# Super-step 0's transposed blocks from VectorE, and super-step 1's key products moved forward

## The chip, the cores and the metric

One core of one Trainium2 chip. The metric is the device time of the whole program in microseconds (us). The kernel before took 1152.81 us, the median of three runs (1151.03 to 1156.87).

## The reference

Three layers, one after the other. The first is a delta-rule attention with a state per batch and head (4 x 8 heads, 768 steps, head size 48):

```
k_n = k / (norm(k) + 1e-6)
for t in range(768):
    y[t]  = q[t] @ state
    v_old = k_n[t] @ state
    state = state + beta[t] * outer(k_n[t], v[t] - v_old)
```

The second takes the 3072 x 384 result through `relu(x @ w_in)**2 @ w_out` (inner size 2048), the third through `(silu(x @ w_gate) * (x @ w_val)) @ w_out2` (inner size 1536). The weights come as float64; the rest is float32.

## The kernel before, in words

The 768 steps are cut into 6 super-steps `J` of 128 steps, each of two chunks `c` of 64; of the four batches two lie on the two halves of the partitions and two are the halves `p` of the free axis, with 8 heads each. Inside a chunk the recurrence becomes a triangular system: `gram` products of the keys with themselves give M, an inverse of I+M is made, and products with it give `u`, from which come the outputs `y` and the next state (`ku`, `ks`). After super-step 0 a first expert loop (`moe1_h`, `moe1_o`, 16 rounds `m` for a super-step) runs on its 512 rows, and the work of the next super-step is put in between by a list of due times (`plan`, `spread`, `slot`).

Super-step 0 and the first part of super-step 1 are written out by hand (L1035 to L1135). The order of the `run(...)` lines is the order on TensorE, VectorE, ScalarE, GpSimd and SyncE (SP), whose queues are served in order. The names there:

- `gram0` (L392) makes the key products: 16 fp32 products a call. `gc` copies those of super-step 0; for super-step 1, `mb0` (L400, GpSimd) makes mask times beta in one of two buffers, `m0` (L407, VectorE) multiplies the product into it, `mout` sends it to memory, `tload` loads it back as T, and `inv` inverts T on GpSimd.
- For super-step 0, `din` brings the 32x32 blocks into T, `inv0` (L522, VectorE) inverts their 16x16 blocks, and `dout` (L430) transposes the result to ND, with the keys' rows on the partitions again.
- `dt` (L568) makes the transposed 16x16 blocks of ND by products with an identity: 32 products a call, four calls, one ScalarE copy each. `d1` and `d2` (L580, L590) merge two 16x16 blocks to a 32x32 inverse: 32 products a call each, a copy after `d1`, four small copies after `d2` that alternate between ScalarE and VectorE. `t11`, `m1`, `m2` then merge two 32x32 blocks to 64x64 (16 products a call); `dcopy` puts the blocks in place; `vn` scales v.
- `amm` makes the query-key products, `amask` (L487) masks them out of PSUM on VectorE.
- `sq` and `root` make the key norms of super-step 1.
- `conv(n)` does n steps of the conversion of an expert weight piece from float64: three VectorE steps a piece (L185, L187, L192), then a high part on ScalarE (L205) and a low part (L208). The low part of a piece is issued when the next piece is complete, or when it is needed. `PRE` is the count of steps done ahead of the loop; inside it the count aimed at is `PRE + int(3 * 0.65 * clock)`, with the clock counting two for a round.
- 20 products of a zero tile (L1082) run on TensorE while VectorE inverts.

PSUM banks in the start come from `bank(p)`: three of the pool `ps_a` for p = 0, three of `ps_t` for p = 1.

Of the kernel before, what the change touches and what calls it, by code (L numbers as in the profile page):

```python
# [8 lines left out]
F32 = mybir.dt.float32  # L9
F32R = mybir.dt.float32r  # L10
I32 = mybir.dt.int32
ACTF = mybir.ActivationFunctionType
# [9 lines left out]
def delta_attention_moe_moe2_kernel(  # L22
# [37 lines left out]
    nc = tc.nc  # L60
# [22 lines left out]
    ps_h = ctx.enter_context(tc.tile_pool(name="ps_h", bufs=2, space=bass.MemoryType.PSUM))  # L83
# [10 lines left out]
    lower = ap.tile([128, 1], F32, name="lower")  # L94
# [13 lines left out]
    own_w = wp.tile([128, 4 * DM], F32, tag="w", name="ND")  # L108
    own_h, own_l = (xp.tile([128, KD, TOK], F32, tag=t, name="own").rearrange("p k t -> p (k t)") for t in ("xh", "xl"))
    ND, BM = (t[:, 0:1024].rearrange("p (x t) -> p x t", t=32) for t in (own_w, own_l))  # L110
    ident = own_l[:, 1024:1152]
    tick = own_h[:, 512:640]
    TD = [t.rearrange("p (u h t) -> p u h t", u=2, h=8) for t in (own_w[:, 1024:1536], own_h[:, 0:512])]
    KB = {}
    T = ap.tile([128, 32, 32], F32, name="T")
    TMP = ap.tile([128, 240], F32, name="TMP")
# [44 lines left out]
    class Piece:  # L161
# [20 lines left out]
        def run(self):  # L182
            if is64:
                f, fi = self.f, self.f.bitcast(I32)
                nc.vector.tensor_scalar(out=fi, in0=fi, scalar1=3, scalar2=None, op0=ALU.logical_shift_left)  # L185
                yield
                nc.vector.scalar_tensor_tensor(  # L187
                    out=self.d[:, 1], in0=self.d[:, 1], scalar=-0x80000000, in1=fi,
                    op0=ALU.bitwise_and, op1=ALU.bitwise_or,
                )  # L190
                yield
                nc.vector.scalar_tensor_tensor(  # L192
                    out=self.d[:, 1], in0=self.d[:, 0], scalar=29, in1=self.d[:, 1],
                    op0=ALU.logical_shift_right, op1=ALU.bitwise_or,
                )
            yield
# [29 lines left out]
    def load_w1(pc, kd, eng=nc.sync):  # L226
        if (pc, kd) != LAST:
            load_piece((w_in, w_out)[kd], pc, kd == 1, raw1[pc, kd], eng)
            loaded[pc, kd, 0] = raw1[pc, kd]
# [92 lines left out]
    def bank(p, shape, name):  # L322

        if startup and p == 0:
            return ps_a.tile(shape, F32, tag="a", name=name)
        return ps_t.tile(shape, F32, tag="t", name=name)
# [88 lines left out]
    TT = T.rearrange("x t s -> x s t")  # L415
# [13 lines left out]

    def d_out():  # L430
        nc.vector.transpose(out=ND.rearrange("s x t -> s t x"), in_=T)

    def d_rest():

        for b0 in (32, 96):
            nc.gpsimd.memset(NTT[b0:b0 + 32, :, 0:32], 0.0)
        c_ = NTT[:, :, 32:64]
        nc.gpsimd.tensor_tensor(c_, c_, bF.unsqueeze(2).to_broadcast([128, 32, 32]), op=ALU.mult)
# [123 lines left out]
                )  # L562

    t11 = {}
    d_t = {}


    def d_tr(c, p):  # L568

        ps = bank(p, [128, 8, 16], "ps_dt")  # L570
        n = ND[:, 16 * c + 8 * p:16 * c + 8 * p + 8]
        for h in range(8):
            for b0 in range(0, 128, 32):
                nc.tensor.matmul(
                    ps[b0:b0 + 32, h], n[b0:b0 + 16, h], ident[b0:b0 + 16, b0:b0 + 16], start=True, stop=True
                )
        t = TD[c][:, p]
        nc.scalar.activation(out=t[:, :, 0:16], in_=ps, func=ACTF.Copy)
        d_t[c, p] = t

    def d_merge1(c, p):
        ps = bank(p, [128, 8, 16], "ps_d")
        t, n = d_t[c, p], ND[:, 16 * c + 8 * p:16 * c + 8 * p + 8]
        for h in range(8):
            for b0 in range(0, 128, 32):
                nc.tensor.matmul(ps[b0:b0 + 32, h], n[b0:b0 + 16, h], t[b0:b0 + 16, h, 0:16], start=True, stop=True)

        nc.scalar.activation(out=t[:, :, 16:32], in_=ps, func=ACTF.Copy, scale=lower)

    def d_merge2(c, p):  # L590
        ps = bank(p, [128, 8, 16], "ps_e")
        t, n = d_t.pop((c, p)), ND[:, 16 * c + 8 * p:16 * c + 8 * p + 8]
        for h in range(8):
            for b0 in range(0, 128, 32):
                nc.tensor.matmul(
                    ps[b0:b0 + 16, h], t[b0:b0 + 32, h, 16:32], n[b0:b0 + 32, h, 16:32], start=True, stop=True
                )
        for b0 in range(0, 128, 32):
            copy(b0 // 32 % 2, n[b0:b0 + 16, :, 16:32], ps[b0:b0 + 16])

    def copy(i, out, in_):

        if startup and i:
            nc.vector.tensor_copy(out, in_)
        else:
            nc.scalar.activation(out=out, in_=in_, func=ACTF.Copy)

    def tr11(J, c, p):
        t = TD[0][:, p] if J == 0 and c else ap.tile([128, 8, 32], F32, tag="tq", bufs=2, name="tq")
        if J == 0:  # L610
            ps = bank(p, [128, 8, 32], "ps_tq")
            for h in range(8):
                for b0 in (0, 64):
                    nc.tensor.matmul(
                        ps[b0:b0 + 32, h], ND[b0:b0 + 32, 16 * c + 8 * p + h], ident[b0:b0 + 32, b0:b0 + 32],
                        start=True, stop=True,
                    )
            for b0 in (0, 64):
                copy(b0 // 64, t[b0:b0 + 32], ps[b0:b0 + 32])
            t11[c, p] = t  # L620
            return
        for b0 in (0, 64):
            nc.vector.transpose(out=t[b0:b0 + 32], in_=NT[c][p][b0:b0 + 32, :, 0:32])
        t11[c, p] = t
# [137 lines left out]
    def do_y(J, c, p):  # L762
# [10 lines left out]
        "vn": (v_scale, 0),  # L773
        "nback": (n_back, 0), "t11": (tr11, 0), "m1": (merge1, 0.4), "m2": (merge2, 0.5), "ks": (ks, 0.8),
        "agram": (a_gram, 0.8), "u": (uu, 0.8), "ku": (do_ku, 0.8), "y": (do_y, 0.9),
        "fetch": (fetch_x, 0.01), "dt": (d_tr, 0), "d1": (d_merge1, 0.8), "d2": (d_merge2, 0.8),
        "sq": (k_squares, 0), "root": (k_root, 0), "gram0": (gram0, 0.9), "mb0": (mb0, 0), "m0": (m0, 0),
        "amm": (lambda J, c, p: a_gram(J, c, p, split=True), 0.8), "amask": (a_mask, 0),
        "gc": (g_copy, 0), "brows": (b_rows, 0), "din": (d_in, 0), "dout": (d_out, 0), "drest": (d_rest, 0),
# [223 lines left out]
    def run_all(names):  # L1003
        for n in names:
            run(n)
# [15 lines left out]
    def conv(n, lo=nc.vector):  # L1021

        conv_to(converted() + n, lo)

    P2 = range(2)
    WARM = 20
    mark = ap.tile([128, 1], F32, name="mark")

    def stage(w, J, c):
        run_all((w, J, c, p) for p in P2)  # L1030

    def merge16(w, c):
        run_all((w, c, p) for p in P2)
# [7 lines left out]
        out=BM, in_=BM, compare_op=ALU.is_gt, fill=0.0, base=0, pattern=[[1, 32], [-1, 32]], channel_multiplier=0  # L1041
    )
    nc.gpsimd.memset(AQT[32:64, :, 1], 0.0)
    nc.gpsimd.memset(tick, 0.0)
    run(("loadq", 0))
    run_all(("kt", 1, c) for c in P2)
    run_all(("kb", 1, c) for c in P2)
# [7 lines left out]
    for b0 in (0, 64):  # L1055
        nc.gpsimd.affine_select(
            out=mask[b0:b0 + 64], in_=mask[b0:b0 + 64], compare_op=ALU.is_ge, fill=1.0,
# [12 lines left out]
    run(("brows",))  # L1070
    run(("din",))
    stage("amm", 0, 0)
    run(("sq", 1, 0, 0))
    run(("inv0", range(14, 6, -1)))

    nc.vector.reduce_sum(lower, ident.rearrange("p (b z k) -> p z b k", z=2, k=16)[:, 1], axis=AX.XY)
    if WARM:

        nc.vector.memset(tick[:, 0:1], 0.0)
        spare = ps_h.tile([128, 128], F32, tag="h", name="ps_w")  # L1080
        for _ in range(WARM):
            nc.tensor.matmul(spare, tick, tick, start=True, stop=True)  # L1082
    run(("inv0", range(6, 0, -1)))

    nc.gpsimd.tensor_copy(mark, T[:, 0, 0:1])
    run(("dout",))
    merge16("dt", 0)
    stage("amask", 0, 0)
    run(("drest",))
    merge16("dt", 1)  # L1090
    run(("sq", 1, 0, 1))
    run(("sq", 1, 1, 0))
    merge16("d1", 0)
    run_all(("gram0", 1, 0, p) for p in P2)
    merge16("d1", 1)
    run(("sq", 1, 1, 1))
    merge16("d2", 0)
    run(("root", 1))
    run_all(("mb0", 1, 0, p, nc.gpsimd) for p in P2)
    merge16("d2", 1)  # L1100
    run(("vn", 0, 0, nc.vector))
    stage("t11", 0, 0)
    run(("dcopy", 0))
    run_all(("m0", 1, 0, p) for p in P2)
    run_all(("mout", 1, 0, p) for p in P2)
    stage("t11", 0, 1)
    run_all(("gram0", 1, 1, p) for p in P2)
    run_all(("mb0", 1, 1, p, nc.gpsimd) for p in P2)
    stage("m1", 0, 0)
    stage("m1", 0, 1)  # L1110
    stage("m2", 0, 0)
    run_all(("m0", 1, 1, p) for p in P2)
    run_all(("mout", 1, 1, p) for p in P2)
    run_all(("tload", 1, c) for c in P2)
# [1 line left out]
    load_w1(5, 0)  # L1116
    load_w1(5, 1)
    run(("inv", 1, 0, 1, nc.gpsimd))
    stage("m2", 0, 1)
    stage("u", 0, 0)  # L1120
    run(("dcopy", 1))
    conv(1)
    stage("amm", 0, 1)
    stage("y", 0, 0)
    conv(2)
# [174 lines left out]
```

## Time and profile before

| | |
|---|---|
| median of three runs | 1152.81 us |
| profiled execution | 1150.16 us |
| its span | 1148.4 us |
| TensorE busy | 1077.1 us (94%) |
| VectorE busy | 616.2 us (54%) |
| ScalarE busy | 383.0 us (33%) |
| GpSimd busy | 235.1 us (20%) |
| mean granted TensorE clock | 0.957 of full speed |

The profile is of one execution. Its page gives busy times, 40 slices of the span and the chain that ended last; the trace behind it is asked for one stretch, engine or line at a time. PE is TensorE's matmul, PEld its weight load, DVE VectorE, ACT ScalarE, POOL GpSimd, SP SyncE; L568 is line 568 of the kernel. Times of day are us from the start of the span. A busy engine is not an engine at its peak, and the idle time of an engine off the critical path costs nothing. "issue" is time in which an engine waited for nothing that the profile shows.

### The profile page before, as it was taken

Reading aid. Unit: us, or ns where it says so; the run is one execution under the profiler, and the core shown is the slowest. Engines: PE = TensorE matmul, PEld = TensorE weight load, DVE = VectorE, ACT = ScalarE, POOL = GpSimd, SP = SyncE. Lnnn points to the kernel's source line nnn. Section 1 sums busy time; section 2 is a strip of 40 time slices with the busy share of each in tenths; the row PEclk is TensorE's granted clock in tenths of the full one; section 3 lists DMA queues with packets and bytes.
Section 4 is the critical chain, followed back from the end, with each engine's and each line's share of the span. In section 5 each row is a group of like instructions: output and inputs, shape, how many; then the busy total and the mean of one; then the engine's idle time right before and its main releaser. Section 6 shows DMA issues by size and latency. Waiting matters only on the chain.

```text
span 1148.4 us, 24956 instructions
## 1 busy us (share of the span) xinstructions
PE 1077.1 (94%) x10887; PEld 893.9 (78%) x10887; DVE 616.2 (54%) x1026; ACT 383.0 (33%) x687; POOL 235.1 (20%) x368
## 2 busy tenths in 40 slices
PE   3686779999999999999999999999999999999998
PEld 3685557778887888888888787888888888888887
DVE  5468697566557547555543699534333343343333
ACT  2133464342233234223333687322122221222212
POOL 3129500851381085138000000000000000000000
PEclk7668789999999999999999999999999999999999
DMA  9344603262343316232211467001010010000000
GB/s 295 133 93 147 159 1 69 62 173 54 65 120 89 77 46 157 56 67 67 69 30 29 166 192 246 3 1 55 1 55 1 1 55 1 23 33 1 28 1 27
DMA packets 116924, 84.53 MB, mean 74 GB/s; under 512 B 91472, under 2 KB 95440, under 8 KB 116816
## 3 DMA queue, kind: packets, MB, share of 16 engines
q1 hardware_dynamic: 115616, 77.97, 24.8%
q0 software_dynamic: 1056, 4.72, 1.1%
q8 instruction: 85, 1.39, 0.5%
q10 hardware_dynamic: 144, 0.26, 0.1%
q14 instruction: 23, 0.19, 0.0%
HBM read 61.70 MB, written 21.23 MB: 72 GB/s over the span
## 4 chain that ended last, share of the span: by engine, by line
PE 71%; issue 11%; DVE 8%; POOL 4%; DMA 3%; ACT 3%; SPq 0%; POOLq 0%; DVEq 0%; ACTq 0%
PE ps_o L991 13%; PE ps_v L966 12%; PE ps_g L966 12%; PE ps_h L873 10%; PE ps_y L899 10%; PE ps_g L386 2%; PE ps_u L663 2%; POOL T L517 1%; POOL TMP L510 1%; PE ps_a L478 1%; DVE raw L187 1%; PE ps_k L655 1%; PE ps_m L632 1%; DVE w L208 1%; DMA raw<-in_moe_w_val_dram 1%
## 5 line engine op out<-in xcount | busy, mean ns | idle before, releaser
L873 PE MATMUL ps_h<-xh,w 128*128 128x512 f32 (+1 forms) x636 | 205.9, 384 | 8.4 <-DVE w L208 7.9
L899 PE MATMUL ps_y<-hh,w 128*128 128x512 f32 (+1 forms) x606 | 158.4, 398 | 1.9 <-DVE w L208 1.8
L966 PE MATMUL ps_g<-x2h,w 128*128 128x512 f32 x432 | 144.8, 389 | 0.0
L966 PE MATMUL ps_v<-x2h,w 128*128 128x512 f32 x432 | 144.7, 389 | 0.0
L873 PEld LDWEIGHTS ps_h<-xh,w 128*128 128x128 f32 x636 | 118.0, 191 | 32.8 <-DVE w L208 9.4
L970 DVE SCALAR_TENSOR_TENSOR th<-th,ps_g 128x512 f32<-128x512 f32 x72 | 49.5, 687 | 169.1 <-ACT th L969 169.0
L876 ACT ACTIVATE r<-ps_h 128x512 f32<-128x512 f32 (+1 forms) x106 | 58.8, 555 | 220.0 <-PE ps_h L873 204.6
L899 PEld LDWEIGHTS ps_y<-hh,w 128*128 128x128 f32 x606 | 110.3, 194 | 25.2 <-DVE w L208 2.3
L879 DVE TENSOR_TENSOR r<-r 128x512 f32<-128x512 f32 (+1 forms) x72 | 50.3, 699 | 134.8 <-ACT hh L877 134.5
L873 PE MATMUL ps_h<-xl,w 128*128 128x512 f32 (+1 forms) x318 | 119.7, 376 | 1.9 <-DVE xl L736 1.3
L991 PE MATMUL ps_o<-ph,w 128*128 128x512 f32 x432 | 111.9, 389 | 1.3 <-ACT ye L915 1.3
L510 POOL TENSOR_TENSOR TMP<-T 128x30 f32<-128x30 f32 (+9 forms) x150 | 87.0, 580 | 83.4 <-DMA T<-m_scr 68.5
L969 ACT ACTIVATE th<-ps_g 128x512 f32<-128x512 f32 x72 | 43.0, 597 | 175.7 <-PE ps_g L966 175.6
L883 DVE TENSOR_TENSOR hl<-r,hh 128x512 fp32r<-128x512 f32 (+1 forms) x106 | 75.7, 714 | 40.6 <-ACT r L881 35.1
L991 PEld LDWEIGHTS ps_o<-ph,w 128*128 128x128 f32 x432 | 81.0, 188 | 18.5 <-ACT ye L915 1.8
L517 POOL TENSOR_TENSOR T<-T,TMP 128x30 f32<-128x30 f32 (+9 forms) x150 | 92.5, 617 | 11.4
L966 PEld LDWEIGHTS ps_g<-x2h,w 128*128 128x128 f32 x432 | 81.1, 188 | 17.1 <-ACT hh L877 0.3
L966 PEld LDWEIGHTS ps_v<-x2h,w 128*128 128x128 f32 x432 | 81.1, 188 | 16.8
L973 ACT ACTIVATE ph<-th 128x512 fp32r<-128x512 f32 x72 | 45.5, 631 | 134.1 <-DVE th L971 134.1
L899 PE MATMUL ps_y<-hl,w 128*128 128x512 f32 (+1 forms) x303 | 84.2, 387 | 5.7 <-DVE hl L883 5.6
L966 PE MATMUL ps_v<-x2l,w 128*128 128x512 f32 x216 | 84.0, 389 | 0.0
L966 PE MATMUL ps_g<-x2l,w 128*128 128x512 f32 x216 | 84.0, 389 | 0.0
(155 smaller groups left out, 1729.3 us busy)
## 6 DMA issues: line engine op xcount, KB each, us to landing
raw<-in_moe_w_out_dram SPq DMA_DIRECT2D x13, 768.0 KB, 6.3
raw<-in_moe_w_in_dram SPq DMA_DIRECT2D x8, 768.0 KB, 12.0
KT<-in_kt_dram SPq DMA_DIRECT2D x12, 448.0 KB, 8.9
m_scr<-M SPq DMA_DIRECT2D x20, 256.0 KB, 2.5
KB<-in_kn_dram SPq DMA_DIRECT2D x12, 384.0 KB, 8.2
AQ<-in_q_dram SPq DMA_DIRECT2D x12, 384.0 KB, 7.1
V<-in_v_dram SPq DMA_DIRECT2D x12, 384.0 KB, 3.9
raw<-in_moe_w_gate_dram SPq DMA_DIRECT2D x6, 768.0 KB, 4.5
```

Source lines behind the costliest of these rows:

```text
L510: eng.tensor_tensor(tmp[:, r0:r1], t_[:, r0:r1, kk:kk + 1].to_broadcast([n, r1 - r0, w]), t_[:, kk:kk + 1, kk + 1:].to_broadcast([n, r1 - ...
L517: eng.tensor_tensor(t_[:, r0:r1, kk + 1:], t_[:, r0:r1, kk + 1:], tmp[:, r0:r1], op=ALU.add)
L873: nc.tensor.matmul(ps, w_[:, kk], x_[:, kk, cols], start=n == 0, stop=n == 3 * KD - 1)
L876: nc.scalar.activation(out=r, in_=ps, func=ACTF.Relu)
L879: nc.vector.tensor_tensor(r, r, r, op=ALU.mult)
L883: eng.tensor_tensor(hl[:, at], r, hh[:, at].bitcast(F32), op=ALU.subtract)
L899: nc.tensor.matmul(acc[f], w_[:, fs], h_, start=first, stop=m == NM1 - 1 and n == 2)
L966: nc.tensor.matmul(ps, w_[:, kk], x_[:, kk], start=n == 0, stop=n == 3 * KD - 1)
L969: nc.scalar.activation(out=th, in_=gp, func=ACTF.Tanh, scale=0.5)
L970: nc.vector.scalar_tensor_tensor(out=th, in0=th, scalar=1.0, in1=gp, op0=ALU.add, op1=ALU.mult)
L973: nc.scalar.activation(out=hh, in_=th, func=ACTF.Copy)
L991: nc.tensor.matmul(o_acc[J][f], w_[:, fs], h_, start=m == 0 and n == 0, stop=m == NM2 - 1 and n == 2)
```

## The change

`dout` makes a second transposition on VectorE, which gives the transposed blocks (NDT) directly, and `dt` with its products and copies is gone; `d1` reads NDT. The 20 warm-up products are gone. The four `gram0` calls of super-step 1 stand behind `amm`, ahead of the inverse. `mb0`, `m0`, `mout`, `tload`, three weight loads and `inv` of super-step 1 stand further forward; `amask`, `dcopy` and `vn` further back. Three conversion steps are put ahead of `u` and one behind it is gone. The diff, without renamed parts:

```diff
     def d_out():
         nc.vector.transpose(out=ND.rearrange("s x t -> s t x"), in_=T)
+        nc.vector.transpose(out=NDT.rearrange("t x s -> t s x"), in_=TT)
...
-    def d_tr(c, p):
-        ps = bank(p, [128, 8, 16], "ps_dt")
-        n = ND[:, 16 * c + 8 * p:16 * c + 8 * p + 8]
-        for h in range(8):
-            for b0 in range(0, 128, 32):
-                nc.tensor.matmul(
-                    ps[b0:b0 + 32, h], n[b0:b0 + 16, h], ident[b0:b0 + 16, b0:b0 + 16], start=True, stop=True
-                )
-        t = TD[c][:, p]
-        nc.scalar.activation(out=t[:, :, 0:16], in_=ps, func=ACTF.Copy)
...
     def d_merge1(c, p):
...
-                nc.tensor.matmul(ps[b0:b0 + 32, h], n[b0:b0 + 16, h], t[b0:b0 + 16, h, 0:16], start=True, stop=True)
-        nc.scalar.activation(out=t[:, :, 16:32], in_=ps, func=ACTF.Copy, scale=lower)
+                nc.tensor.matmul(ps[b0:b0 + 32, h], n[b0:b0 + 16, h], nt[b0:b0 + 16, h, 0:16], start=True, stop=True)
+        nc.scalar.activation(out=t[:, :, 0:16], in_=ps, func=ACTF.Copy, scale=lower)
...
     stage("amm", 0, 0)
+    for c in P2:
+        run_all(("gram0", 1, c, p) for p in P2)
     run(("sq", 1, 0, 0))
-    run(("inv0", range(14, 6, -1)))
     nc.vector.reduce_sum(lower, ...)
-    if WARM:
-        nc.vector.memset(tick[:, 0:1], 0.0)
-        spare = ps_h.tile([128, 128], F32, tag="h", name="ps_w")
-        for _ in range(WARM):
-            nc.tensor.matmul(spare, tick, tick, start=True, stop=True)
-    run(("inv0", range(6, 0, -1)))
+    run(("inv0", range(14, 0, -1)))
     run(("dout",))
-    merge16("dt", 0)
-    stage("amask", 0, 0)
     run(("drest",))
-    merge16("dt", 1)
+    merge16("d1", 0)
     run(("sq", 1, 0, 1))
     run(("sq", 1, 1, 0))
-    merge16("d1", 0)
-    run_all(("gram0", 1, 0, p) for p in P2)
     merge16("d1", 1)
     run(("sq", 1, 1, 1))
-    merge16("d2", 0)
     run(("root", 1))
     run_all(("mb0", 1, 0, p, nc.gpsimd) for p in P2)
-    merge16("d2", 1)
-    run(("vn", 0, 0, nc.vector))
-    stage("t11", 0, 0)
-    run(("dcopy", 0))
+    merge16("d2", 0)
     run_all(("m0", 1, 0, p) for p in P2)
     run_all(("mout", 1, 0, p) for p in P2)
-    stage("t11", 0, 1)
-    run_all(("gram0", 1, 1, p) for p in P2)
     run_all(("mb0", 1, 1, p, nc.gpsimd) for p in P2)
-    stage("m1", 0, 0)
-    stage("m1", 0, 1)
-    stage("m2", 0, 0)
+    merge16("d2", 1)
+    stage("amask", 0, 0)
+    stage("t11", 0, 0)
     run_all(("m0", 1, 1, p) for p in P2)
     run_all(("mout", 1, 1, p) for p in P2)
     run_all(("tload", 1, c) for c in P2)
     load_w1(4, 1)
     load_w1(5, 0)
     load_w1(5, 1)
     run(("inv", 1, 0, 1, nc.gpsimd))
+    run(("dcopy", 0))
+    run(("vn", 0, 0, nc.vector))
+    stage("t11", 0, 1)
+    stage("m1", 0, 0)
+    conv(2)
+    stage("m1", 0, 1)
+    stage("m2", 0, 0)
     stage("m2", 0, 1)
+    conv(1)
     stage("u", 0, 0)
     run(("dcopy", 1))
-    conv(1)
     stage("amm", 0, 1)
```

## Rows read from the trace of the kernel before

**Rows 1.** The page, its parts 1 (busy us, instructions) and 3 (queue: packets, MB).
```profile
PE 1077.1 (94%) x10887; PEld 893.9 (78%) x10887; DVE 616.2 (54%) x1026; ACT 383.0 (33%) x687; POOL 235.1 (20%) x368
...
q8 instruction: 85, 1.39, 0.5%
```

**Rows 2.** TensorE's waits, 28 to 300 us: total us, times, longest.
```profile
PE ps_h L873 <- DVE w L208: 7.9, 3, 5.0
PE ps_m L632 <- issue: 7.2, 1, 7.2
```

**Rows 3.** TensorE's waits, 190 us to the end.
```profile
PE ps_y L899 <- DVE hl L883: 5.6, 5, 2.8
```

**Rows 4.** The chain of waits, 0 to 200 us: start, us, what.
```profile
39.94 2.16 issue
42.09 0.29 PE ps_dt L574 x10
...
43.82 2.22 issue
...
52.34 1.70 issue
...
55.34 2.43 issue
57.77 0.81 PE ps_e L595 x50
...
67.61 3.39 PE ps_m L632 x122
...
74.40 3.26 PE ps_u L663 x58
```

**Rows 5.** Windows of 2 us: busy us and count by engine, PEclk, DMA, GB/s.
```profile
42.00:44.00 2.00, 1.72 (x127) 1.61 (x127) 0.85 (x2) 1.36 (x4) 0.00 (x0) 0.65 0.04 8
...
54.00:56.00 2.00, 1.30 (x128) 1.20 (x128) 0.86 (x3) 0.86 (x4) 0.00 (x0) 0.50 0.04 8
```

**Rows 6.** Windows of line L386 alone (one of its two lines).
```profile
46.30:50.10 3.80, 3.67 (x32) 3.48 (x32) 0.50 0.02 4
```

**Rows 7.** Windows: busy us and count by engine, PEclk, DMA share, GB/s.
```profile
19.40:30.40 11.00, 0.00 (x0) 0.00 (x0) 10.83 (x40) 0.83 (x2) 0.00 (x0) 0.50 1.04 401
61.80:80.00 18.20, 18.20 (x509) 17.95 (x511) 11.16 (x24) 7.29 (x16) 2.08 (x2) 0.50 0.36 75
80.20:90.00 9.80, 6.94 (x256) 6.13 (x254) 6.51 (x11) 2.80 (x4) 5.41 (x12) 1.00 0.89 273
```

**Rows 8.** VectorE in order of time: start, us (of the group), line, operation, count.
```profile
33.60 1.95 DVE L431 STREAM_TRANSPOSE ND<-T 128x1024 f32<-128x1024 f32 x1
35.38 2.81 DVE L496 TENSOR_TENSOR AQ<-ps_a,mask 64x512 f32<-64x512 f32 x4
...
60.57 1.01 DVE L318 TENSOR_TENSOR V<-V,nB 128x768 f32<-128x768 f32 x1
...
63.19 0.85 DVE L604 COPY NT<-ND 32x512 f32<-32x512 f32 x2
64.08 1.29 DVE L409 SCALAR_TENSOR_TENSOR M<-ps_g,M 128x512 f32<-128x512 f32 x2
...
112.87 0.98 DVE L185 TENSOR_SCALAR f<-f 128x768 int32<-128x768 int32 x1
113.88 1.21 DVE L187 SCALAR_TENSOR_TENSOR raw<-raw,f 128x768 int32<-128x768 int32 x1
...
157.46 0.88 DVE L623 STREAM_TRANSPOSE tq<-NT 32x256 f32<-32x256 f32 x2
```

**Rows 9.** ScalarE in order of time; in brackets idle time and who ended it.
```profile
55.00 0.56 ACT L606 ACTIVATE ND<-ps_e 16x128 f32<-16x128 f32 x2 [0.35 <-DVE ND L604]
```

**Rows 10.** GpSimd in order of time.
```profile
69.64 1.04 POOL L402 TENSOR_TENSOR M<-mask,bB 128x512 f32<-128x512 f32 x1 [1.35 <-DMA m_scr<-M]
...
129.95 0.16 POOL L519 MEMSET T<- 128x32 f32 x1
```

More of the change, by code (lines that the diff above doesn't have):

```diff
@@ L111, in delta_attention_moe_moe2_kernel @@
     ident = own_l[:, 1024:1152]
-    tick = own_h[:, 512:640]
-    TD = [t.rearrange("p (u h t) -> p u h t", u=2, h=8) for t in (own_w[:, 1024:1536], own_h[:, 0:512])]
+    NDT = own_h[:, 0:1024].rearrange("p (x t) -> p x t", t=32)
+    TD = [t[:, 1024:1536].rearrange("p (u h t) -> p u h t", u=2, h=8) for t in (own_w, own_h)]
     KB = {}
@@ L564, in delta_attention_moe_moe2_kernel, with d_merge1, d_merge2 @@
     t11 = {}
-    d_t = {}
-    def d_tr(c, p):
-        ps = bank(p, [128, 8, 16], "ps_dt")
-        n = ND[:, 16 * c + 8 * p:16 * c + 8 * p + 8]
+    def d_merge1(c, p):
+        ps = bank(p, [128, 8, 16], "ps_d")
+        x = slice(16 * c + 8 * p, 16 * c + 8 * p + 8)
+        t, n, nt = TD[c][:, p], ND[:, x], NDT[:, x]
+        for h in range(8):
+            for b0 in range(0, 128, 32):
+                nc.tensor.matmul(ps[b0:b0 + 32, h], n[b0:b0 + 16, h], nt[b0:b0 + 16, h, 0:16], start=True, stop=True)
+        nc.scalar.activation(out=t[:, :, 0:16], in_=ps, func=ACTF.Copy, scale=lower)
+    def d_merge2(c, p):
+        ps = bank(p, [128, 8, 16], "ps_e")
+        t, n = TD[c][:, p], ND[:, 16 * c + 8 * p:16 * c + 8 * p + 8]
         for h in range(8):
@@ L574, in d_tr @@
                 nc.tensor.matmul(
-                    ps[b0:b0 + 32, h], n[b0:b0 + 16, h], ident[b0:b0 + 16, b0:b0 + 16], start=True, stop=True
-                )
-        t = TD[c][:, p]
-        nc.scalar.activation(out=t[:, :, 0:16], in_=ps, func=ACTF.Copy)
[L579 to L583, printed above, removed]
-        for h in range(8):
-            for b0 in range(0, 128, 32):
-                nc.tensor.matmul(ps[b0:b0 + 32, h], n[b0:b0 + 16, h], t[b0:b0 + 16, h, 0:16], start=True, stop=True)
-        nc.scalar.activation(out=t[:, :, 16:32], in_=ps, func=ACTF.Copy, scale=lower)
[L590 to L594, printed above, removed]
-                nc.tensor.matmul(
-                    ps[b0:b0 + 16, h], t[b0:b0 + 32, h, 16:32], n[b0:b0 + 32, h, 16:32], start=True, stop=True
+                    ps[b0:b0 + 16, h], t[b0:b0 + 32, h, 0:16], n[b0:b0 + 32, h, 16:32], start=True, stop=True
                 )
@@ L775, in delta_attention_moe_moe2_kernel @@
         "agram": (a_gram, 0.8), "u": (uu, 0.8), "ku": (do_ku, 0.8), "y": (do_y, 0.9),
-        "fetch": (fetch_x, 0.01), "dt": (d_tr, 0), "d1": (d_merge1, 0.8), "d2": (d_merge2, 0.8),
+        "fetch": (fetch_x, 0.01), "d1": (d_merge1, 0.8), "d2": (d_merge2, 0.8),
         "sq": (k_squares, 0), "root": (k_root, 0), "gram0": (gram0, 0.9), "mb0": (mb0, 0), "m0": (m0, 0),
@@ L1025, in delta_attention_moe_moe2_kernel @@
     P2 = range(2)
-    WARM = 20
     mark = ap.tile([128, 1], F32, name="mark")
@@ L1043, in delta_attention_moe_moe2_kernel @@
     nc.gpsimd.memset(AQT[32:64, :, 1], 0.0)
-    nc.gpsimd.memset(tick, 0.0)
     run(("loadq", 0))
```

## The prediction

> **What bounds the kernel now.** I read the page's first lines, then TensorE's waits by stretch, then the chain of waits through the start, then VectorE's and GpSimd's instructions in order of time. From 190 us on TensorE hardly waits: its longest total is 5.6 us over 958 us [rows 3]. There the end is TensorE's own work, and whatever makes super-step 0 reach that stretch earlier comes off the end one for one. What can be shortened lies before it: the start, until the products `u` begin at 74.40 [rows 4], and the first expert loop, where TensorE waits 7.9 us for converted weights and once 7.2 us before `ps_m` [rows 2].
>
> In the start the chain shows something that isn't a data wait: stops named "issue" of 2.16, 2.22, 1.70 and 2.43 us [rows 4], in the midst of groups of equal, independent products. TensorE goes on at 42.10 and 46.04, and at 54.04 and 57.77: 3.94 and 3.73 us apart; between 46.04 and 54.04 lie two such steps of 4.0. A window between two stops holds 127 or 128 matmul records, at 8 GB/s over 2 us, so 16 KB [rows 5]. The instruction queue moved 85 packets, 1.39 MB, for 10887 matmul and 10887 weight-load records [rows 1]: 16 KB and 256 instructions each. I read from this that TensorE's instructions come in blocks of 128 records, which is 64 of the code's fp32 products (each leaves two records), and that the next block comes about 3.95 us after the one before. The small products of a block take 1.30 us [rows 5], so in the start TensorE is paced by the count of products, not by their size or by its clock.
>
> The Trainium skill ("Runtime: NRT & Kernel Launch", section on instruction fetch mechanics) agrees on blocks of 16 KiB and 256 instructions, but holds the fetch to be mostly hidden behind execution. This trace doesn't agree for products this small. By the page's rule the start would run at the products' own times; what that would give is the second rival.
>
> **The change, part by part.** Times are those of the profiled execution: 1150.16 us, span 1148.4. The median of the three runs is 1152.81, 2.65 more, and that is added at the end.
>
> *Transposed blocks.* `d_tr` goes: 4 calls of 32 products, 128 in all, two blocks; four ScalarE copies go too. Added is one more VectorE transposition of 128x1024. The row of the first is 33.60 for 1.95 [rows 8]. The new one reads and writes with strides; the trace has no such row. From below I bound it by 1.0 (half), from above by 3.9 (twice), and take 1.95, the row of the same size and type. `d1` can then start at 33.60 + 3.90 = 37.5, just where the removed products started before.
>
> *Warm-up and gram products.* 20 warm-up products go. The 64 `gram0` products of super-step 1 move behind `amm`: there TensorE stands still from 19.4 to 30.4 [rows 7], and 32 of them took 3.67 us [rows 6], so 7.4 us in a hole that now lasts to 37.5. Cost nothing; if the keys came 10 us late it would still be nothing. Off the path behind the inverse go 128 + 64 = 192 products, three blocks, 11.9 us of fetch.
>
> *To the end of `d2`.* The stop at 39.94 left 10 of the 256 records of `d_tr` undone [rows 4], so it came after 64 + 32 + 20 + 123 = 239 products, so blocks end at 175, 239, 303, 367. In the changed order 160 products lie before `d1`, and `d1` and `d2` are products 160 to 416. Entering the blocks at 37.9, 41.9, 45.8 and 49.8, the last 49 products end about 50.8. Before, `d2` ended at 57.77 + 0.81 = 58.6 [rows 4]. Gain 7.8.
>
> *VectorE then takes over.* The copies of `d2` alternate between ScalarE and VectorE, about 0.3 us each, the one waiting for the other [rows 9]; eight of them end at 52.6. Then in VectorE's queue: `amask`, which before lay in its idle time at 35.38 and costs 2.81 [rows 8], to 55.4; two `t11` copies at 0.42 (half of the 0.85 row), to 56.25; two `m0`, 1.29, to 57.55; `dcopy` 0.85 and `vn` 1.01, to 59.4; two more `t11` copies, to 60.25 [rows 8]. Before, that point was at 64.08 + 1.29 + 0.8 = 66.2. So `amask` and the second `m0` take back 2 us. But before, `m1` began only at 67.61, behind gram products, and took 3.39; it and `m2` fill the 6.8 us to `u` [rows 4]. Now the first half of `m1` is done by then; the second half runs from 59.85 for 1.7; VectorE copies the first half's results (0.85), does the two new conversion steps (0.56 + 1.09 where nothing disturbs them, I take 1.65) and copies again, to 63.6; the second half of `m2` ends near 65.1, where `u` begins. Against 74.40: **9.3 us sooner.** Bounds: 3 (each group waits in full for the copies of the one before, below) and 13 (no fetch limit).
>
> *The added wait.* `m0` of the second chunk now stands ahead of `dcopy`, `vn`, `t11` and all of `m1` in VectorE's queue. It waits for `mb0` on GpSimd, and that for M of the first chunk to land, since there are two buffers. Before, the second `mb0` ended at 70.68, 5.3 us after the first chunk's `m0` (65.37) [rows 8, 10]. Now that `m0` runs behind the first `d2` copies, about 48.3 to 49.6, so `mb0` ends near 54.9, 1.3 us before VectorE wants it at 56.25. Nothing, but with little to spare.
>
> *M and the inverse forward.* SP gives out M, the loads of T and three weight pieces earlier; the queue has nothing else then. GpSimd's inverse ended at 129.95 [rows 10] and VectorE first touches its result at 157.46 [rows 8]: 27.5 us of slack. Ending it sooner is worth nothing by itself. It takes GpSimd away from the expert loop's start, where VectorE's conversion steps run long beside it; I don't count that apart.
>
> *Conversions.* The list has 2+1+2+2+2+2 = 11 steps ahead of the loop where there were 1+2+2+2+2 = 9, and the loop's pace counts on from there. The longest wait, 5.0 [rows 2], is TensorE waiting while VectorE does steps L185 and L187 (0.98 + 1.21 [rows 8]), then the third step and the low part. Two steps done, it falls by 2.2. The other waits on weights, 2.9 together, can vanish: 5.1 at most. But the 7.2 us before `ps_m` come from VectorE's backlog, so part comes back there. I take 4.0; bounds 0 and 7.
>
> *Sum.* 9.3 + 4.0 = 13.3. 1150.16 - 13.3 = 1136.9; with 2.65 for the median **1139.5 us**. Its own range is 1134 to 1145.
>
> **The rivals.**
>
> *The loop gives its part back.* VectorE has the same list from the loop's start to `ps_m`; if it is the limit throughout, the waits on weights only move into the 7.2. For it: that wait is the largest of all single ones. Against: VectorE itself idles while TensorE waits. Only the 9.3 remain: 1143.5. Chance 0.17.
>
> *Fetch is hidden after all.* Then `d1` and `d2` (four blocks of 1.30 us and what their copies need) end near 45 and the square-root chain and copies near 48.3, and VectorE's list runs on from there: 4.3 us more than forecast, 1135.2. Against: the stops sit inside groups without any data wait. For it: a long wait of TensorE ahead of `d1` may let it get further ahead than I count. Chance 0.10.
>
> *Banks run short.* `amm` and the gram products now hold four of the six PSUM banks of `ps_a` and `ps_t` until `amask` and the second `m0`, so each `d1`, `d2` and `t11` call waits for the copy of the call before. If that adds to the fetch instead of lying beside it, eight calls lose 0.4 to 1.2 us each, some 6: 1145.5, up to 1149. Against: there are 4 us per block and copies take 0.4 to 1.3. Chance 0.10.
>
> *Slower: the clock stays low.* Before, it was 0.50 from 61.8 to 80.0 with TensorE busy without a gap (18.20 of 18.20), and 1.00 from 80.2 [rows 7]. The change takes the gram products out of that stretch and breaks it by waits on VectorE, and the warm-up is gone. If the rise (from 1.2 to 2.4 GHz) then comes only in the expert loop, the work from `y` to the loop runs low: 6.94 us busy in 80.2 to 90 [rows 7] and about as much again to 103, up to 14 more if all of it doubles, and some 3 in the first loop rounds: 1139.5 + 17 = 1156.5. It decides from 13 us of loss on, so only if nearly every product there takes twice as long. Against: 32 gram products took 3.67 us at 0.50 [rows 6] and the rows at 80.2 have VectorE busy for 6.51 of 9.8. The Trainium skill ("TensorE: Matmul & The Clock Gate", Part 1) says that the throttled level is the default and activity releases it, which speaks for this rival; the trace agrees so far that the level was low until a long unbroken run. Chance 0.07.
>
> **How the numbers follow.** Forecast 0.56, rivals 0.17, 0.10, 0.10, 0.07. A measurement of this kernel can tell about 0.5%, 5.8 us, from no change. Faster by that (below 1147.0): forecast, the first two rivals, and part of the third, less a few misjudged sizes: 0.82. Within it: the rest of the third and half of the fourth: 0.12. Slower: 0.06. The range takes in the fetch rival and most of the bank rival: 1131 to 1149.
>
> **What would show it.** `d1` starting at 37.5 without warm-up before it, stops still about 3.95 us apart, `d2` ending near 51; `amask` on VectorE between `d2` and `t11`; `u` starting near 65; the wait on L208 of 5.0 down to about 2.8; a low clock until `u`. Wrong would be: the added transposition above 3.9; `m0` waiting for GpSimd by more than 2 us; stops that shrink to nothing; `u` after 70; or a wait before super-step 1's `ps_m` of more than 11 us.

## The result: 1131.55 us, 1.7% faster, and the profile after

The changed kernel takes 1131.55 us, the median of four runs (1130.44 to 1134.66), against 1152.09 (1151.03 to 1156.87) of the kernel before on the same chip: a ratio of 0.9831, 95% interval 0.9804 to 0.9857. The forecast was 1139.5, with a range of 1131 to 1149. The profiled execution is the one of 1130.44, with a span of 1128.7 us and a mean granted clock of 0.960; it is 19.7 us under the one before, where the sum of the prediction said 13.3.

Four places of the two traces show where this comes from. The first column is the kernel before; `d2` ends and `u` starts there as in [rows 4].

| | before | after | moved by |
|---|---|---|---|
| `d2` ends | 58.6 | 48.7 | -9.9 |
| `u` starts | 74.40 | 64.46 | -9.9 |
| first expert product | 103.48 | 95.22 | -8.3 |
| first `ps_m` of super-step 1 | 165.12 | 147.04 | -18.1 |
| end of the span | 1148.4 | 1128.7 | -19.7 |

So the start gives 9.9, 1.7 of that is lost on the way to the expert loop, the loop up to `ps_m` gives 9.8, and 1.6 comes later.

TensorE and the instruction queue, from the page: two packets and 296 matmul records fewer than in [rows 1] (148 products: 128 of `dt`, 20 warm-up).

```profile
PE 1061.7 (94%) x10591; PEld 881.4 (78%) x10591; DVE 610.4 (54%) x1026; ACT 381.0 (34%) x683; POOL 232.4 (21%) x367
...
q8 instruction: 83, 1.36, 0.5%
```

TensorE's waits of the kernel after from 26 to 300 us (total us, times, longest). The wait for weights, 7.9 in [rows 2], is 3.1; that before `ps_m` grew from 7.2 to 8.4. The first row, the wait for VectorE's inverse, has nothing to do in it any more.

```profile
PE ps_d L575 <- DVE own L433: 15.6, 1, 15.6
PE ps_m L621 <- issue: 8.4, 1, 8.4
...
PE ps_h L862 <- DVE w L209: 3.1, 2, 2.5
```

From 175 us to the end it waits as little as in [rows 3]:

```profile
PE ps_y L888 <- DVE hl L872: 5.6, 6, 2.4
```

TensorE in order of time through `d1` and `d2` (start, us of the group, line, operation, count; in brackets its idle time and who ended it). The stops named "issue" are still there. TensorE goes on from these at 40.74, 44.19 and 47.66, so 3.45 and 3.47 apart; before it was 3.7 to 4.0 [rows 4]. Between the stops lie 157, 128, 128 and 99 records.

```profile
37.01 2.32 PE L575 MATMUL ps_d<-own,ND 16*32 16x16 f32 x157 [15.64 <-DVE own L433]
40.74 1.51 PE L575 MATMUL ps_d<-own,ND 16*32 16x16 f32 x98 [1.41 <-issue]
...
44.19 1.04 PE L584 MATMUL ps_e<-ND 32*16 32x16 f32 x99 [1.71 <-issue]
...
47.66 1.05 PE L584 MATMUL ps_e<-ND,own 32*16 32x16 f32 x99 [1.17 <-issue]
```

VectorE in order of time (start, us of the group, line, operation, count): the second transposition, `amask` behind `d2`, the second `m0`, the second of the two conversion steps between the halves of `m1`, the copy behind them, and the end of a conversion in the loop.

```profile
34.99 1.88 DVE L433 STREAM_TRANSPOSE own<-T 128x1024 f32<-128x1024 f32 x1
...
50.38 2.81 DVE L498 TENSOR_TENSOR AQ<-ps_a,mask 64x512 f32<-64x512 f32 x4
...
54.42 1.29 DVE L410 SCALAR_TENSOR_TENSOR M<-ps_g,M 128x512 f32<-128x512 f32 x2
...
59.81 0.96 DVE L188 SCALAR_TENSOR_TENSOR raw<-raw,f 128x768 int32<-128x768 int32 x1
62.13 0.77 DVE L593 COPY ND<-ps_m 32x256 f32<-32x256 f32 x2 [1.37 <-ACT ND L595]
...
103.93 1.18 DVE L193 SCALAR_TENSOR_TENSOR raw<-raw 128x768 int32<-128x768 int32 x1
105.03 1.12 DVE L209 TENSOR_TENSOR w<-raw,w 128x768 fp32r<-128x768 f32 x1
```

The copy at 62.13 waited for ScalarE, which had a step of the conversion ahead of its own copy (from 61.72):

```profile
60.80 0.90 ACT L180 ACTIVATE f<-raw 128x768 f32<-128x768 f32 x1 [2.38 <-DVE raw L188]
```

GpSimd: the second `mb0`, and the first and last instruction of super-step 1's inverse, which before began at 83.72 and ended at 130.1 [rows 10].

```profile
52.31 2.04 POOL L403 TENSOR_TENSOR M<-mask,bB 128x512 f32<-128x512 f32 x2 [5.25 <-DMA m_scr<-M]
...
65.55 0.94 POOL L512 TENSOR_TENSOR TMP<-T 128x30 f32<-128x30 f32 x1 [11.20 <-DMA T<-m_scr]
...
109.35 0.16 POOL L521 MEMSET T<- 128x32 f32 x1
```

**The loop, read by windows.** A window from the first expert product to `ps_m` holds the same work of TensorE in every kernel here, 240 or 241 matmul records. Its rows give length, TensorE's busy time and count, granted clock, DMA share and GB/s. The kernel before, with stretches inside it:

```profile
103.48:165.12 61.64, 43.27 (x240) 0.86 0.40 102
114.00:118.00 4.00, 0.29 (x1) 0.54 1.04 191
118.00:122.00 4.00, 4.00 (x12) 0.61 1.04 261
...
132.00:133.00 1.00, 0.00 (x0) 1.00 0.26 102
135.00:136.00 1.00, 1.00 (x4) 0.50 0.65 106
```

The kernel after, with the stretch at its longest wait for weights and the one behind:

```profile
95.22:147.04 51.82, 39.01 (x241) 0.91 0.45 111
...
106.00:110.00 4.00, 3.79 (x10) 0.61 0.55 194
110.00:114.00 4.00, 4.00 (x18) 0.97 0.49 158
```

Idle time fell from 18.4 to 12.8 us: the waits for weights from 9.7 (7.9 at `h`, 1.8 at `y`) to 3.1, less 1.2 given back before `ps_m`. The other 4.3 us are busy time: as many records take less of it. In the four us at 118 before, TensorE is busy throughout and finishes 12 records; in the four at 110 after, 18. The clock stood near its lower level (0.50 is 1.2 GHz, 1.00 is 2.4) there, right behind the wait of 5.0 us. Before there are three such low stretches in the loop, behind the waits of 5.00, 1.84 and 2.48 us (products go on at 117.70, 127.77 and 133.90; between the last two the clock is back at 1.00, at 132, and low again at 135); after there is one.

### The profile page after: what moved, and what is told of

The parts are those of the page before. It is cut to its first block, busy times and chain, and to the rows that moved or that the text cites. A ratio compares the mean times of both kernels' runs of the same rounds, so it can differ in the third digit from the quotient of the medians.

```text
span 1128.7 us, 24358 instructions
## 1 busy us (share of the span) xinstructions
PE 1061.7 (94%) x10591; PEld 881.4 (78%) x10591; DVE 610.4 (54%) x1026; ACT 381.0 (34%) x683; POOL 232.4 (21%) x367
## 4 chain that ended last, share of the span: by engine, by line
PE 80%; DVE 8%; issue 3%; POOL 3%; DMA 3%; ACT 2%; SPq 0%; DVEq 0%; POOLq 0%; ACTq 0%
PE ps_h L862 15%; PE ps_y L888 15%; PE ps_o L980 13%; PE ps_g L955 13%; PE ps_v L955 13%; PE ps_u L652 2%; PE ps_g L387 2%; PE ps_a L480 2%; POOL T L519 1%; PE ps_k L644 1%; POOL TMP L512 1%; PE ps_m L621 1%; PE ps_y L676 1%; PE ps_x L633 1%; PE ps_s L664 1%
## 5 line engine op out<-in xcount | busy, mean ns | idle before, releaser
L888 PE MATMUL ps_y<-hh,w 128*128 128x512 f32 (+1 forms) x606 | 156.0, 393 | 0.0
L868 DVE TENSOR_TENSOR r<-r 128x512 f32<-128x512 f32 (+1 forms) x72 | 46.9, 651 | 138.8 <-ACT hh L866 138.4
L980 PEld LDWEIGHTS ps_o<-ph,w 128*128 128x128 f32 x432 | 81.0, 188 | 18.4 <-ACT ye L904 1.7
```

Of the source, the lines that this page charges most:

```text
L868: nc.vector.tensor_tensor(r, r, r, op=ALU.mult)
L888: nc.tensor.matmul(acc[f], w_[:, fs], h_, start=first, stop=m == NM1 - 1 and n == 2)
L980: nc.tensor.matmul(o_acc[J][f], w_[:, fs], h_, start=m == 0 and n == 0, stop=m == NM2 - 1 and n == 2)
```

## The experiments

Places are read from TensorE's rows in each profiled execution; there `u` of the kernel before starts at 74.33. "Ratio" is against the kernel before on the same chip, with its 95% interval. The runs of the changed kernel lie within 4.2 us of each other, so between two variants two or three us aren't told apart by the median; places in the trace are steadier. The loop is the same in the kernel after, e4, e5 and e6, and takes 51.5 to 52.5 us there; in the kernel before, e3 and e7, which have neither the two steps ahead nor the early inverse, it takes 60.8 to 63.1.

### What the loop's 9.8 us are

**The conversion steps put back** (e1_conv_back): all else as in the kernel after.

```diff
     stage("m1", 0, 0)
-    conv(2)
     stage("m1", 0, 1)
...
-    conv(1)
     stage("u", 0, 0)
     run(("dcopy", 1))
+    conv(1)
```

> The changed kernel with 9 conversion steps ahead of the expert loop instead of 11, placed as before. Theory A (the two steps ahead are what shortened the loop, by taking TensorE's waits on weights and VectorE's idle time out): the first expert product stays within 1 us of 95.2, the longest wait of ps_h on the low part goes from 2.5 back to 4.5 to 5, the stretch from the first expert product to super-step 1's first ps_m grows from 51.8 us by 4 to 6, time 1135 to 1138. Theory B (the loop is shorter because GpSimd's inverse ends earlier and no longer slows VectorE): that stretch grows by 1 at most, time 1131 to 1133.

Measured: 1138.96 us (1138.72 to 1140.37), ratio 0.9887, 0.9863 to 0.9912. `u` starts 0.9 sooner than in the kernel after and the first expert product 2.4 sooner, but the loop takes 60.65 instead of 51.82. Its longest wait for weights is back at 4.2 (waits, then windows as above):

```profile
PE ps_h L862 <- DVE w L209: 7.5, 3, 4.2
```

```profile
92.86:153.51 60.65, 43.66 (x241) 0.86 0.45 107
96.00:100.00 4.00, 4.00 (x13) 0.58 0.10 12
108.00:112.00 4.00, 4.00 (x10) 0.50 1.02 226
124.00:128.00 4.00, 4.00 (x14) 0.67 0.87 124
```

The steps do more than I said: 8.8 us in the loop, of which 4.2 are idle time and 4.65 the same 241 records at a lower clock, in three low stretches.

**The inverse late** (e2_inv_late): GpSimd gets super-step 1's inverse only behind `ku`, held there by a small copy that needs the state. It then runs from 78.39 to 130.8, much as in the kernel before.

```diff
-    run(("inv", 1, 0, 1, nc.gpsimd))
...
     stage("ku", 0, 0)
+    nc.gpsimd.tensor_copy(mark[64:112], RS[0][64:112, 0, 0, 0:1])
+    run(("inv", 1, 0, 1, nc.gpsimd))
```

> The changed kernel with GpSimd's inverse of super-step 1 held back to about 78 us (65.6 before) by one small copy that reads the state, so that it ends about 27 us after the first expert product, as in the kernel before. Theory B: VectorE's busy time between the first hl and the second t11 transposition goes from 39.3 back to about 42.8, the stretch from the first expert product to ps_m grows by 3 to 5, time 1134.5 to 1136.5. Theory A: it grows by 1 at most, time 1131 to 1133.

Measured: 1137.42 us (1135.87 to 1141.14), ratio 0.9876, 0.9846 to 0.9906; the loop takes 56.41, 4.6 more than in the kernel after. VectorE's groups of 95 to 150 us show why (count, total busy us, mean ns of one, idle before). The kernel after:

```profile
L188 DVE SCALAR_TENSOR_TENSOR raw<-raw,f 128x768 int32<-128x768 int32 x10 | 9.8, 980 | 0.3
L193 DVE SCALAR_TENSOR_TENSOR raw<-raw 128x768 int32<-128x768 int32 x9 | 8.8, 983 | 0.2
L209 DVE TENSOR_TENSOR w<-raw,w 128x768 fp32r<-128x768 f32 x9 | 8.7, 969 | 0.0
L872 DVE TENSOR_TENSOR hl<-r,hh 128x512 fp32r<-128x512 f32 x9 | 6.3, 697 | 7.4 <-ACT r L870 7.4
L186 DVE TENSOR_SCALAR f<-f 128x768 int32<-128x768 int32 x10 | 5.7, 572 | 0.0
```

and with the late inverse:

```profile
L188 DVE SCALAR_TENSOR_TENSOR raw<-raw,f 128x768 int32<-128x768 int32 x10 | 10.7, 1068 | 0.3
L193 DVE SCALAR_TENSOR_TENSOR raw<-raw 128x768 int32<-128x768 int32 x9 | 10.6, 1174 | 0.2
L209 DVE TENSOR_TENSOR w<-raw,w 128x768 fp32r<-128x768 f32 x9 | 10.0, 1109 | 0.0
L872 DVE TENSOR_TENSOR hl<-r,hh 128x512 fp32r<-128x512 f32 x9 | 7.7, 850 | 6.2 <-ACT r L870 6.2
L186 DVE TENSOR_SCALAR f<-f 128x768 int32<-128x768 int32 x10 | 6.7, 673 | 0.0
```

The same 47 instructions take 45.7 us instead of 39.3. In the kernel after, L193 and L209 take 1.18 and 1.12 at 103.9 and 105.0, beside GpSimd, and 0.95 each from 111.6 on, once the inverse has ended; with the late inverse they are back at 0.95 from 132.1 on. The longest wait for weights is 2.9, and there are two low stretches, one behind it and one at 122:

```profile
95.82:152.23 56.41, 41.24 (x241) 0.91 0.40 100
```

```profile
122.00:126.00 4.00, 4.00 (x12) 0.61 0.00 0
```

So both theories hold, and they aren't a sum: of the loop's 61.64 us, the steps alone (this run) take 5.2, the early inverse alone (the run before) 1.0, both 9.8. The 1.0 is within the spread of the kernels with neither part.

### What the start's 9.9 us are

**More products behind the inverse** (e4_more_behind): `d1` of chunk 1 is written three times, 128 small products more than the kernel after has.

```diff
+        for rep in range(3 if c == 1 else 1):
             for h in range(8):
```

> The changed kernel with the d1 products of the second chunk written three times over: 128 small products more, between d1 and d2, result unchanged. If instruction blocks pace TensorE: two blocks, d2 ends near 55.7 instead of 48.7 and u begins 6 to 7 us later, with stops about 3.5 us apart, time about 1138. If the products' own time does: 2.6 to 3.8 us, time about 1134.5.

One time, 1138.55 us, span 1136.9. `d2` ends at 56.67 and `u` starts at 72.42, both 8.0 later than in the kernel after; the end comes 8.2 later. The chain of waits shows full blocks of 128 records, each 1.90 us of work, and a stop behind each:

```profile
38.73 2.23 issue
40.96 1.90 PE ps_d L576 x128
42.87 1.55 issue
44.42 1.90 PE ps_d L576 x128
46.32 1.83 issue
```

They go on 3.46 and 3.73 us apart, and 128 products are two blocks, 4.0 us each. Had only the products' own time counted it would have been 3.8.

**The same number in the hole** (e5_more_in_hole): 64 small products ahead of each of the last two `gram0` calls, 128 in all, in TensorE's idle time ahead of `d1`.

```diff
     def gram0(J, c, p, ...):
...
+        if (J, c) == (1, 1):
+            ps, k = g0[J, c, p], KT[J, c][:, p]
+            for rep in range(2):
+                for h in range(8):
+                    for b0 in range(0, 128, 32):
+                        nc.tensor.matmul(ps[b0:b0 + 32, h, 0:16], k[b0:b0 + 16, h, 0:32], k[b0:b0 + 16, h, 0:16], ...)
```

> The changed kernel with 128 more small products (16x32 by 16x16, overwritten afterwards) ahead of the gram products of super-step 1's second chunk, in TensorE's hole ahead of d1. If instruction blocks pace only what lies behind the inverse, two more blocks in the hole cost nothing: TensorE is idle again well before d1, d1 starts within 1 us of 37.0, d2 ends within 1 us of 48.7, time 1130 to 1133. If a product costs wherever it stands (position of the blocks, clock), d2 ends 2 us later or more.

One time, 1133.63 us. `d1` starts at 36.86, `u` at 64.44 (64.46 in the kernel after): free. The instruction queue moves 85 packets here and in the run before, 83 in the kernel after. What was taken out and moved paid because it stood behind the inverse, not because it was work.

**The warm-up kept** (e6_warm_kept): the 20 products of the zero tile again, and 44 small ones in the hole, which with them make one block, so that the blocks behind fall as in the kernel after.

```diff
...
-    run(("inv0", range(14, 0, -1)))
+    run(("inv0", range(14, 6, -1)))
+    nc.vector.memset(tick[:, 0:1], 0.0)
...
+    for _ in range(20):
+        nc.tensor.matmul(spare, tick, tick, start=True, stop=True)
+    run(("inv0", range(6, 0, -1)))
```

> The changed kernel with the 20 warm-up products kept, ahead of d1, and 44 small ones in the hole so that the instruction blocks end at the same products. If the start is paced by instruction blocks and not by the clock: granted clock near 1.0 at d1, d2 ends within 1 us of 48.7, time 1130 to 1133. If the low clock costs something there: d2 and u 1.5 to 3 us sooner, time 1128 to 1130.

Measured: 1132.89 us (1130.29 to 1134.26), ratio 0.9846, 0.9821 to 0.9872, not told apart from the kernel after. The granted clock is 1.00 from 34 to 40 us and 0.50 from 41 to 50. TensorE's first two groups, as shown above for the kernel after:

```profile
36.42 1.62 PE L583 MATMUL ps_d<-own,ND 16*32 16x16 f32 x157 [0.44 <-DVE own L441]
40.28 1.52 PE L583 MATMUL ps_d<-own,ND 16*32 16x16 f32 x98 [2.23 <-issue]
```

Windows (busy us and count of PE, PEld, DVE, ACT, POOL, then the clock), first of this run:

```profile
37.00:50.00 13.00, 6.18 (x491) 5.61 (x480) 6.65 (x22) 4.55 (x15) 2.04 (x2) 0.62 0.29 79
```

and of the kernel after:

```profile
37.00:50.00 13.00, 7.00 (x529) 6.55 (x531) 6.88 (x21) 4.53 (x15) 2.46 (x3) 0.50 0.22 59
```

At the full clock the first 157 records take 1.62 us instead of 2.32, and the stop behind them 2.23 instead of 1.41. From the start of `d1` to the end of `d2` it is 11.8 us, in the kernel after 11.7, so the clock doesn't set the pace there. `u` starts 1.0 sooner, at 63.48, of which 0.6 are an earlier `d1`.

**Only the transposed blocks from VectorE** (e3_dt_only): the kernel before without `dt`.

```diff
         nc.vector.transpose(out=ND.rearrange("s x t -> s t x"), in_=T)
+        nc.vector.transpose(out=NDT.rearrange("t x s -> t s x"), in_=TT)
...
-    merge16("dt", 0)
...
-    merge16("dt", 1)
```

> The kernel before with only the transposed blocks taken from VectorE, everything else in its old place. If instruction blocks pace TensorE in the start: 128 products less are two blocks, d2 ends near 51 to 52 instead of 58.6 and u begins near 67 to 68 instead of 74.4, time about 1145 (1143.5 to 1146.5). If TensorE is paced by the products' own time and the copies: 2.6 to 4 us less, time 1148 to 1149.5.

Measured: 1143.70 us (1141.50 to 1145.77), ratio 0.9932, 0.9905 to 0.9958. `u` starts at 65.25, 9.1 sooner than before, where two blocks are worth 8: three blocks begin before `d2` ends (41.74, 45.29, 48.85) where it was five, and they are 3.6 apart, not 3.7 to 4.0. The loop takes 63.10, as before or a little more: all of this part's gain is in the start.

**Only the key products forward** (e7_gram_only): the kernel before with `gram0` of super-step 1 behind `amm`; the tile of the warm-up products moves to another PSUM pool.

```diff
     stage("amm", 0, 0)
+    for c in P2:
+        run_all(("gram0", 1, c, p) for p in P2)
...
-    run_all(("gram0", 1, 0, p) for p in P2)
...
-    run_all(("gram0", 1, 1, p) for p in P2)
```

> The kernel before with only super-step 1's gram products moved ahead of the inverse. Block theory: 64 products less behind the inverse and 7.3 us of their own time, of which one block (4 us) lies in the stretch of d1 and d2 and the rest ahead of m1: d2 ends near 54.5, u begins near 68 to 69, time 1145 to 1147. If VectorE's queue sets the start instead, u begins after 71 and the time is 1148 to 1150.

Measured: 1144.19 us (1142.48 to 1148.77), ratio 0.9940, 0.9921 to 0.9958. `u` starts at 66.9, 7.4 sooner. The two parts alone are 9.1 and 7.4, together 9.9: they overlap. In the kernel after VectorE has one gap of 0.44 us between 50.38 and 60.77 (`amask`, copies, `m0`, two steps), so it is what would be late next; the two runs that take the two steps out of it, e1 and v4, have `u` 0.9 and 1.0 sooner.

### Versions beyond the change

**Low parts on GpSimd sooner** (v1_low_pool).

```diff
-        N1 = 9
+        N1 = 3
```

> The changed kernel with the low parts of the weights computed on GpSimd from round 3 of the expert loop instead of round 9. If VectorE's list is what delays super-step 1's ps_m (8.4 us of wait): VectorE's busy time before it falls by 5 or 6 pieces of 0.95 us, the wait by 3 to 5, time 1127 to 1129. If GpSimd's slower low parts (1.0 to 1.6 us each) become the wait of ps_h instead, or slow VectorE beside them, time 1131 to 1134.

Measured: 1135.73 us (1135.44 to 1137.31), ratio 0.9876, 0.9854 to 0.9899. The loop takes 53.10; the wait before `ps_m` is 10.4 instead of 8.4. The shorter wait that I expected isn't there.

**Two more steps early** (v2_conv_front): `conv(2)` also ahead of the second half of `d1`, where VectorE is idle; 13 steps in all.

```diff
     run(("sq", 1, 1, 0))
-    merge16("d1", 1)
     run(("sq", 1, 1, 1))
+    conv(2)
+    merge16("d1", 1)
```

> The changed kernel with two further conversion steps ahead of the loop, 13 in all, put into VectorE's idle time between d1 and d2 (behind the last key squares). Theory A: two more steps shorten the stretch from the first expert product to ps_m again by 2 to 5, at no more than 1 us in the start, time 1127 to 1130. If what the two steps of the change gained was only the first long wait, which is now 2.5, the stretch falls by 1 at most: 1130.5 to 1132.5.

Measured: 1135.37 us (1135.25 to 1137.55), ratio 0.9876, 0.9850 to 0.9902. The loop falls to 49.52, with no wait for weights over 1.4, but its first product comes at 98.17, 3 later, and one wait from 140 us on is new:

```profile
PE ps_y L888 <- DVE w L209: 6.1, 1, 6.1
```

**The two steps moved** (v4_conv_moved): as v2, without the two between the halves of `m1`.

```diff
     stage("m1", 0, 0)
-    conv(2)
     stage("m1", 0, 1)
```

> The changed kernel with its two conversion steps between the m1 products moved into VectorE's idle time between d1 and d2; 11 in all, as there. Without them between m1 and m2, u begins 0.9 us sooner and the first expert product up to 2.4 sooner, as where the steps were taken back; the loop stays at 52: 1129 to 1131. If they delay the root chain and with it the first m0, nothing: 1131 to 1133.

Measured: 1133.27 us (1131.12 to 1135.22), ratio 0.9851, 0.9825 to 0.9877: `u` 1.0 sooner, the loop 50.62, the end not told apart from the kernel after.

**A slower pace of conversion** (v8_slower_pace), in the kernel after:

```diff
-        CR = 0.65
+        CR = 0.5
```

> The changed kernel with the pace of conversion in the loop at 0.5 instead of 0.65 of three steps a count, so that VectorE has fewer steps in its list ahead of super-step 1's transposition. If VectorE's list is what makes TensorE wait 8.4 us for ps_m: the wait falls by 3 to 6 and the time to 1126 to 1129. If TensorE then waits for weights instead: more waits of ps_h on the low part, later ones too, time 1131 to 1135.

Measured: 1152.18 us (1148.12 to 1154.36), ratio 1.0005, 0.9987 to 1.0023: the whole gain is gone. The wait before `ps_m` falls only to 6.3, and the loop takes 57.67:

```profile
PE ps_h L862 <- DVE w L209: 9.7, 4, 3.7
```

and from 200 to 300 us TensorE is idle for 12.4 us at a clock of 0.91, in the kernel after for 2.7 at 0.97.

**The slower pace with the 13 steps** (v6_front_pace): v2 and v8 together.

> 13 steps ahead of the loop and the pace of 0.5 together. If both help and don't overlap: 1122 to 1126. If the pace costs waits on weights, the two steps ahead cover them at least at first: not above the kernel with the pace alone.

Measured: 1134.43 us (1133.12 to 1136.58), ratio 0.9864, 0.9840 to 0.9887. `ps_m` comes at 141.37, 5.7 sooner than in the kernel after, and the end 2.7 later. Of these 8.4 us the windows of ten us from there to 310 show 2.6 as more idle time. The clock is lower in two of them above all (0.83 instead of 1.00 at 180, 0.66 instead of 0.99 at 220); what that costs isn't settled. No version beat the changed kernel.

### The loop in all fourteen kernels

The count of low stretches (windows of one us in a row with a clock below 0.75, between the first expert product and the wait before `ps_m`) orders TensorE's busy time for the same 240 or 241 records:

| low stretches | TensorE busy, us | in |
|---|---|---|
| 0 | 37.4 to 37.7 | v1, v2, v4, v6 |
| 1 | 38.8 to 39.0 | after, e4, e5, e6 |
| 2 | 41.2 to 41.5 | e2, e7, v8 |
| 3 | 43.3 to 44.6 | before, e1, e3 |

From one group to the next the middles rise by 1.4, 2.5 and 2.5 us, beside the wait that it stands behind. Not every wait has one: in v1, v4 and v8 those of 2.56, 2.49 and 2.38 us have none, in the kernel after that of 2.53 has; what decides it isn't shown.

The windows give the clock's share as an estimate: busy time times the part of the clock that was missing, over windows of half a us, is 5.1 us before and 1.7 after, and without it all fourteen kernels lie between 37.3 and 38.4. It takes a record to last twice as long at half the clock; the windows above have 10 records in 4 us at 0.50 and 18 at 0.97. So some 3 of the 4.3 us are the clock; the rest isn't settled.

## Why the prediction came out as it did

The side was right. The sum was not: it gave 13.3 us where 19.7 came, and its own range, 1134 to 1145, didn't hold the time. The stated range did, by half a us, but it reached so low for the rival in which fetch is hidden, and that rival falls; that it held is luck. By its steps:

- **Blocks of instructions: right, with one stop too many.** The stops stay, 3.45 us apart instead of the 3.95 I took, and `d2` ends at 48.7 instead of 50.8. The block ends fall where I put them, but the first, at product 175, stops nothing: TensorE runs 157 records, to product 239, before the first stop, so three blocks begin on the path and not four. That 128 products cost 8.0 behind the inverse and nothing in the hole is shown by e4 and e5, so the rival in which fetch is hidden falls.
- **The added transposition: right.** 1.88 for the 1.95 taken; `d1` starts at 37.01, forecast 37.5.
- **VectorE takes over: right.** `amask` stands where it was put, with its 2.81, and `u` starts at 64.46, forecast 65.1: 9.9 sooner for 9.3. Of the 2.1 us gained at `d2` against the forecast 1.9 are left at VectorE's last `t11` copy (58.4, forecast 60.25); 1.4 go at 62.13, where it waits for ScalarE's copy behind a step of the conversion, which I hadn't counted.
- **The added wait: right.** The second `mb0` ends at 54.35 and `m0` begins at 54.42, no more than 0.1 behind it.
- **Banks: the rival falls.** The stretch of `d1` and `d2` became shorter than forecast, not longer.
- **The clock: lower, but not what the stretch follows.** From `u` to the first expert product the same 641 or 642 records take 2.3 us more busy time (windows of the kernel before, then after):

```profile
74.40:103.48 29.08, 22.04 (x641) 0.78 0.57 158
```

```profile
64.46:95.22 30.76, 24.35 (x642) 0.64 0.35 119
```

  The stretch is 1.7 us longer, a tenth of the fourth rival's 17. But e6 has the clock at 0.71 there, 23.22 us busy, and takes 30.69, as long as the kernel after. The length goes with the count of conversion steps ahead of the loop: 28.7 to 30.3 us in the four kernels with 9 (before, e1, e3, e7), 30.7 to 32.1 in the eight with 11. So most of the 1.7 looks like a price of the two added steps, which my sum left out behind `u`; it wasn't tried by itself.
- **The conversions: the mis-sized term.** "I take 4.0; bounds 0 and 7"; the loop gave 9.8. The mechanism was right: the longest wait fell by 2.5 to 2.5 (forecast 2.8), and 1.2 came back before `ps_m`. Two steps of the working failed. I priced a wait at its own length. Three waits before were followed by low stretches of the clock and only one after; busy time fell by 4.3 us (43.27 to 39.01), some 3 of them by the clock, and my working has no term for that. And I left out the wait of 1.8 at `y`, so the waits gone are 6.6, not at most 5.1.
- **The inverse: wrong beside the two steps.** "Ending it sooner is worth nothing by itself." Its result isn't needed sooner, and without the two steps ahead it brings 1.0 us (e1), which isn't told from nothing. But with them e2 shows 4.6 us of the loop to hang on when it runs, because VectorE's steps are longer beside it (47 instructions, 45.7 us beside 39.3). I named this and didn't count it.

The sum as measured: 9.9 - 1.7 + (6.6 - 1.2 + 4.3) + 1.6 = 19.5; the spans have 19.7, the rest is rounding. The forecast had 9.3 + 4.0. What the 1.6 behind `ps_m` are isn't settled; it is within what two executions differ by. That the steps and the inverse bring more together than one by one is measured, by more than the spread of the loop between kernels that have it alike; the clock's part is an estimate, which follows the count of low stretches (three before and in e1, two in e2, one after), and why each wait falls as it does wasn't traced further.

## What to carry to other kernels

Ask of a group of small products whether it stands behind the last wait or in a hole: 128 of them cost 8.0 us in one place and nothing in the other. Price a wait of TensorE with the low clock that can follow it, and count such stretches from the windows of the trace before. When an engine's work is moved because its result has slack, look at who runs beside it at the old place.

## What the runs showed of the hardware

Behind most of the longer waits in the loop TensorE ran about three us or more at 1.2 GHz (the granted clock 0.50), and as many records took some 1.4 to 2.5 us longer for each such stretch, over fourteen kernels with none to three of them. The Trainium skill ("TensorE: Matmul & The Clock Gate", section on HAM oscillation) describes a kernel that pays the throttled clock anew at every wait for data; these runs agree, but for the waits of 2.56, 2.49 and 2.38 us in v1, v4 and v8.

VectorE's steps took longer while GpSimd inverted: with the late inverse L193 took 1174 instead of 983 ns on average and L209 1109 instead of 969, with 0.95 us for one once GpSimd was done. The Trainium skill ("SBUF — State Buffer", section "Who interferes with whom") says that a VectorE instruction with two inputs in SBUF contends with a GpSimd instruction that reads SBUF; L188, L193 and L209 are such, and agree.

A transposition of 128x1024 with strides on both sides took 1.88 us, one with strides on one side 1.95 [rows 8].
